# Reordering the prologue of a Fourier filter and mixer kernel: inputs first, tables and weights under the transposes, token sums among the roundings

## The chip, the cores and the metric

One core of one Trainium2 chip. The metric is the device time of one execution in microseconds (us); most kernels here ran five times beside runs of the kernel before on the same chip. All runs quoted are fast, with one core at a mean granted TensorE clock of 0.99. A ratio is the mean time of one kernel's fast runs over that of the other's of the same rounds, so it is not quite the ratio of the medians that are quoted. Times inside an execution ("the relu at 159.6") are from the profiled run, counted from the start of its span. In the profile's lines PE is TensorE, PEld its weight loads, DVE VectorE, ACT ScalarE, POOL GpSimd and SP SyncE; a q after the name means the engine's issuing side.

## The reference

```python
def _attn_ref(x, filt_r, filt_i):              # x: 8 x 3008 x 256, float32
    X = np.fft.rfft(x, axis=1)
    Y = X * (filt_r + 1j * filt_i)[None]       # filters: 1505 x 256
    return np.fft.irfft(Y, n=x.shape[1], axis=1).astype(np.float32)

def _moe_ref(x, w_tok1, w_tok2, w_ch1, w_ch2): # weights are float64
    h = np.maximum(x.transpose(0, 2, 1) @ w_tok1, 0.0) @ w_tok2
    u = x + h.transpose(0, 2, 1)
    return (u + np.maximum(u @ w_ch1, 0.0) @ w_ch2).astype(np.float32)
```

## The kernel before

The kernel does the first batch's Fourier filter in a prologue, and in the mixer it does the filters of later batches beside the matmuls. The weights arrive as float64, so each of 40 tiles is rounded to float32 in several steps: ScalarE makes the leading part, VectorE the rest, and the two parts are then added, either by VectorE or by two TensorE matmuls whose sum ScalarE copies out. One `convert()` ends one tile, copies for the next and starts a load for a later one.

```python
    early = [(up, "u")] * 2 + [(tp, "t")] * 2 + [(vp, "v")] * 2
    late = [(t2p, "t2"), (t3p, "t3")]
    stages = [(t4p, "t4")] * (A // 2) + early * 3 + late * 5   # staging buffer of each tile, in order
    ...
    def halves(st, n, pair):
        nc.scalar.activation(out=top, in_=hi_f, func=AF.Copy, scale=2.0 ** -112)
        yield
        ...                                     # four VectorE instructions -> top, rest
    def on_chip(stat, top, rest, n, parts):     # the sum by TensorE, put off by two roundings
        def f(tag=banks[0]):
            nc.tensor.matmul(ps[:, 0:n], stat, top, start=True, stop=False)
            nc.tensor.matmul(ps[:, 0:n], stat, rest, start=False, stop=True)
            for src, dst in parts:
                nc.scalar.copy(out=dst, in_=src(ps))
        behind.append((ended[0] - 1, f))
    def combine(w): ...                         # five GpSimd sums of channel weights
    def convert():
        ended[0] += 1
        while behind and behind[0][0] < ended[0] - 2:
            behind.pop(0)[1]()
        advance(end); advance(copy); advance(begin)
    ...
    # filter step k of the first batch; FB = 3 filter buffers, three parts of each filter by GpSimd's queue
            nc.tensor.matmul(ps, wbs[k // WC][...], t2, start=True, stop=True)
            nc.vector.tensor_tensor(out=p1, in0=ps, in1=fr, op=ALU.mult)
            ...                                 # two more products, then the inverse matmul of step k - 1
    ...
        for i in range(rounds, A // 2 + TC * N2 // NG):    # the last 14 roundings
            convert()
            ...
            if i == A // 2 + BY_PE - 1:
                sum_up()                        # flush the sums put off
                acc = token_sums(0)             # 96 matmuls in one block
        h1s[0] = token_relu(acc)
```

In all that follows each engine takes its instructions in the program's order, and the transfers of a queue stand in the order of the engine that issues them.

## Time and profile before

| | us |
|---|---|
| median of 3 runs | 2590.05 (2589.63 to 2591.91) |
| span of the profiled run | 2587.2 |
| TensorE busy from 222 us on | 2333.4 of 2365 |
| mixer's first matmul | 167.4 |

The mixer is at TensorE's limit from 222 us on, and the prologue ends at 167.4. The prediction below shows the stages and the chain of waits. Timeline columns: start, length, engine, source line, operation, output and input; in brackets how long the engine had been idle and what ended it.

### The profile page before, as it was taken

To read this page: it belongs to the slowest core of one execution; us is meant where nothing else is said; L and a number is where in the kernel's file an instruction comes from. 1 tells how busy PE (TensorE), PEld (TensorE's weight loads), DVE (VectorE), ACT (ScalarE), POOL (GpSimd) and SP (SyncE) were. 2 spreads that over 40 slices of the span, in tenths; PEclk is the share of its full clock that TensorE was granted. 3 is DMA by queue.
4 is the path that set the end of the run, shared out by engine and by line. 5 is a ranking of instruction groups with operands and counts; after the bars stand their busy time and mean duration, and the time that the engine had idled before them with its cause. 6 is when DMAs were issued, how large, how long until landed. Compare 5 with 4: busy or idle time off the path is not lost.

```text
span 2587.2 us, 31459 instructions
## 1 busy us (share of the span) xinstructions
PE 2505.6 (97%) x10952; PEld 2000.9 (77%) x10952; DVE 1816.0 (70%) x3458; ACT 691.2 (27%) x1347; POOL 526.9 (20%) x966
## 2 busy tenths in 40 slices
PE   5989999999999999999999999999999999999998
PEld 2556666788878777888787777788888888888887
DVE  6897888556675888746666788846678577647676
ACT  2433222123221222222321222212222122212222
POOL 3652211111211112112112111121121121211212
PEclk7999999999999999999999999999999999999999
DMA  6964333312232332202232233211232121100001
GB/s 167 232 195 155 109 106 103 106 48 90 90 90 64 88 88 71 80 17 89 90 96 77 75 84 87 80 31 57 90 85 75 50 64 53 25 9 8 17 12 21
DMA packets 151834, 205.20 MB, mean 79 GB/s; under 512 B 34216, under 2 KB 102034, under 8 KB 151676
## 3 DMA queue, kind: packets, MB, share of 16 engines
q1 hardware_dynamic: 81068, 115.65, 15.7%
q0 software_dynamic: 30656, 39.93, 6.4%
q10 hardware_dynamic: 39952, 47.61, 5.7%
q8 instruction: 87, 1.43, 0.2%
q14 instruction: 71, 0.58, 0.1%
HBM read 131.23 MB, written 71.83 MB: 78 GB/s over the span
## 4 chain that ended last, share of the span: by engine, by line
PE 78%; DVE 13%; issue 3%; DMA 3%; ACT 2%; SPq 0%; ACTq 0%; POOL 0%; DVEq 0%; POOLq 0%
PE ps_po L631 26%; PE ps_pg L597 15%; PE ps_pg L613 11%; PE ps_b L540 4%; PE ps_b L557 4%; DVE t L575 3%; DVE hh L575 3%; PE ps_acc L540 2%; PE ps_acc L557 2%; PE ps_acc L494 2%; PE ps_b L562 2%; PE ps_acc L417 2%; DVE u L575 2%; DVE s L575 1%; PE ps_b L470 1%
## 5 line engine op out<-in xcount | busy, mean ns | idle before, releaser
L575 DVE TENSOR_TENSOR hh<-ps_pg,s 128x512 f32<-128x512 f32 (+3 forms) x864 | 482.4, 586 | 624.4 <-ACT s L600 623.8
L676 POOL DMA_DIRECT2D out_dram<-r x757 | 409.8, 550 | 1949.1 <-ACT hh L618 929.0
L618 ACT ACTIVATE hh<-hh 128x512 f32<-128x512 f32 (+1 forms) x576 | 348.0, 621 | 1122.8 <-DVE hh L575 1122.8
L631 PE MATMUL ps_po<-t,wc 128*128 128x256 f32 (+1 forms) x2304 | 535.5, 375 | 5.4 <-DVE t L575 4.6
L631 PEld LDWEIGHTS ps_po<-t,wc 128*128 128x128 f32 x2304 | 434.5, 190 | 132.9 <-issue 53.3
L631 PE MATMUL ps_po<-hh,wc 128*128 128x256 f32 (+1 forms) x1728 | 413.2, 375 | 3.1 <-POOL wc L339 2.8
L597 PE MATMUL ps_pg<-v,wc 128*128 128x256 f32 (+1 forms) x1728 | 413.3, 375 | 0.2
L631 PEld LDWEIGHTS ps_po<-hh,wc 128*128 128x128 f32 x1728 | 327.5, 190 | 42.4 <-POOL wc L339 3.6
L597 PEld LDWEIGHTS ps_pg<-v,wc 128*128 128x128 f32 x1728 | 326.9, 190 | 40.5 <-DVE v L575 3.0
L613 PE MATMUL ps_pg<-u,wc 128*128 128x256 f32 (+1 forms) x1152 | 294.5, 378 | 7.0 <-DVE hh L575 6.5
L575 DVE TENSOR_TENSOR t<-t,hh 128x256 f32<-128x256 f32 (+1 forms) x576 | 242.0, 420 | 19.8
L613 PEld LDWEIGHTS ps_pg<-u,wc 128*128 128x128 f32 x1152 | 216.2, 190 | 43.5 <-DVE hh L575 17.4
L575 DVE TENSOR_TENSOR s<-ps_pg,hh 128x512 f32<-128x512 f32 (+1 forms) x288 | 196.0, 681 | 30.7 <-DVE hh L575 0.9
L575 DVE TENSOR_TENSOR t<-hh 128x512 f32<-128x512 f32 (+1 forms) x288 | 192.7, 669 | 0.6 <-ACT hh L618 0.6
L597 PE MATMUL ps_pg<-u,wc 128*128 128x256 f32 (+1 forms) x576 | 169.9, 377 | 1.6 <-DVE hh L575 1.6
L613 PE MATMUL ps_pg<-v,wc 128*128 128x256 f32 (+1 forms) x576 | 169.2, 375 | 0.0
L600 ACT COPY s<-ps_pg 128x256 f32<-128x256 f32 (+1 forms) x288 | 106.0, 368 | 154.7 <-PE ps_pg L597 151.5
L613 PEld LDWEIGHTS ps_pg<-v,wc 128*128 128x128 f32 x576 | 108.9, 190 | 13.3
L597 PEld LDWEIGHTS ps_pg<-u,wc 128*128 128x128 f32 x576 | 102.7, 191 | 20.3 <-issue 8.8
L540 PE MATMUL ps_b<-t,w 128*128 128x256 f32 x480 | 106.3, 384 | 4.3 <-DMA t<-g_tmp 4.3
L557 PE MATMUL ps_b<-w,h 128*128 128x512 f32 (+1 forms) x232 | 107.8, 587 | 0.0
L540 PEld LDWEIGHTS ps_b<-t,w 128*128 128x128 f32 x480 | 92.2, 192 | 17.9 <-issue 4.0
(102 smaller groups left out, 2251.4 us busy)
## 6 DMA issues: line engine op xcount, KB each, us to landing
g_tmp<-t ACTq DMA_DIRECT2D x128, 192.0 KB
x<-in_x_dram SPq DMA_DIRECT2D x184, 128.0 KB
out_dram<-r POOLq DMA_DIRECT2D x698, 32.0 KB, 1.8
z_tmp<-t ACTq DMA_DIRECT2D x84, 256.0 KB
t<-z_tmp SPq DMA_DIRECT2D x112, 192.0 KB
t<-g_tmp SPq DMA_DIRECT2D x42, 512.0 KB
wb<-wbi_t SPq DMA_DIRECT2D x80, 224.0 KB
filt<-in_filt_r_dram SPq DMA_DIRECT2D x128, 48.0 KB
```

Source lines behind the costliest of these rows:

```text
L417: nc.tensor.matmul(ps, wa0 if b == 0 else wa, xs.pop((b, c)).rearrange("p a d -> p (a d)"), start=True, stop=True)
L494: nc.tensor.matmul(ps[0:KR], wbs[k // WC][:, k % WC, P:], p, start=(i == 0), stop=(i == len(parts) - 1))
L540: nc.tensor.matmul(acc[:, t, :], w1[:, a, ts(t, P)], t4[b, a // TC4][:, a % TC4, :], start=(a == 0 and t == 0), stop=(a == A - 1 and t == ...
L557: nc.tensor.matmul(ps[:, 0:w], h1[:, t, ts(dh, P)], w2[:, t, ds(m * 512, w)], start=(t == 0), stop=False)
L562: nc.tensor.matmul(ps[:, ds(q * P, n)], t4[b, c][:, r, ts(dh, P)], wai[:, 0:n], start=False, stop=(q == 3))
L575: nc.vector.tensor_tensor(out=out, in0=in0, in1=in1, op=op)
L597: nc.tensor.matmul(ps[:, 0:hw], chan[0][:, jp, n, :], mov, start=True, stop=True)
L600: nc.scalar.copy(out=s[:, 0], in_=g[0][:, 0, 0:hw])
L613: nc.tensor.matmul(ps[:, 0:hw], chan[0][:, jp, n, :], mov, start=True, stop=True)
L618: nc.scalar.activation(out=hs, in_=hs, func=AF.Relu)
L631: nc.tensor.matmul(po[i][:, j, 0:hw], chan[1][:, jp, n, :], mov, start=(jp == 0 and first == 1), stop=(jp == JP - 1 and last == 1))
L676: q.dma_start(rows[g, e, :, ds(h * A + 4 * m, n)], blocks[ts(g, CW), h, e, 0:n])
```

## The change

Its intent: transfers idle under the transposes while the inputs ahead of them share the bandwidth with weights. So the inputs go first, in buffers of their own and over two queues; then seven tables; then weights, seven or more ahead. SyncE takes one part of each later filter load. The roundings that ran ahead of the transposes move beside the filter steps. The token sums are cut in eight parts among the last roundings, and TensorE adds twelve of the sixteen second token weight tiles, not six. The core of the diff:

```diff
-BY_PE = 6
-EARLY = 12
+BY_PE = 8
+BESIDE = 13
...
-                q.dma_start(t[lo + j0:lo + j0 + n, i, k - k0:KC, :],
+                (nc.sync if first and j0 and c >= FB else q).dma_start(t[lo + j0:lo + j0 + n, i, k - k0:KC, :],
...
+    round_ = [(p_, t_) for p_, t_ in ((up, "u"), (tp, "t"), (vp, "v"), (t2p, "t2")) for _ in range(2)]
+    stages = [(t4p, "t4")] * 7 + round_ * 3 + [(t2p, "t2"), (t3p, "t3")] * 5
...
-        q = nc.sync if i < EARLY else nc.gpsimd
+        q = nc.sync
...
-        if i < BY_PE:
+        if i < BY_PE or i % 2:
...
-        advance(begin)
+        while begun[0] < len(tiles) and begun[0] < ended[0] + (4 if begun[0] >= len(tiles) - len(LAST) else 7):
+            start()
...
-        where, tag = ((xp, "x"), (tp, "t"), (vp, "v"))[c % 3] if b == 0 else (xp, "x")
+        where, tag = ((xp, "x"), (t1p, "t1"), *round_[0::2])[c // 2] if b == 0 else (xp, "x")
+            q = nc.gpsimd if b == 0 and h else nc.sync
...
-        ahead = 3 * XB if first else XB
+        ahead = NXC if first else XB
+            if first and i < FB:
+                w_load(i)
+                if i == 0:
+                    for c in range(7):
+                        table_load(c)
...
+                if i >= FB:
+                    for _ in range(2 if i < 9 else 1):
+                        start()
...
-            if i == A // 2 + BY_PE - 1:
+            j = 3 * (i - A // 2 - TC * N2 // NG + 9)
+            if j == 0:
                 sum_up()
-                acc = token_sums(0)
+            if 0 <= j < A:
+                acc = token_sums(0, acc, range(j, j + 3))
+        sum_up()
```

More of the change, by code (lines that the diff above doesn't have):

```diff
@@ L34 @@
 KC = 2
-WC = 2
 DT = 256
@@ L225, in filt_double @@
         nc.scalar.copy(out=t[HALF:P, 0], in_=t[0:HALF, 0])
-    early = [(up, "u")] * 2 + [(tp, "t")] * 2 + [(vp, "v")] * 2
-    late = [(t2p, "t2"), (t3p, "t3")]
-    stages = [(t4p, "t4")] * (A // 2) + early * 3 + late * 5
+    round_ = [(p_, t_) for p_, t_ in ((up, "u"), (tp, "t"), (vp, "v"), (t2p, "t2")) for _ in range(2)]
+    stages = [(t4p, "t4")] * 7 + round_ * 3 + [(t2p, "t2"), (t3p, "t3")] * 5
     def stage(n):
@@ L378, in advance, with start @@
             next(s, None)
+    begun = [0]
+    def start():
+        advance(begin)
+        begun[0] += 1
     def sum_up():
@@ L405, in x_load @@
             lo = h * A + c * XC
-            nc.sync.dma_start(t[h * HALF:(h + 1) * HALF, 0:n, :], rows[:, lo:lo + n, :])
+            q = nc.gpsimd if b == 0 and h else nc.sync
+            q.dma_start(t[h * HALF:(h + 1) * HALF, 0:n, :], rows[:, lo:lo + n, :])
             if n < XC:
-                nc.sync.dma_start(t[h * HALF:(h + 1) * HALF, n:XC, :], rows[:, lo:lo + 1, :])
+                q.dma_start(t[h * HALF:(h + 1) * HALF, n:XC, :], rows[:, lo:lo + 1, :])
         xs[b, c] = t
@@ L429, in dft, with table_load @@
         wbs = {}
+        def table_load(c):
+            where, tag = ((xp, "x"), (t1p, "t1"))[(c - 3) // 2] if first and 3 <= c < 7 else (wbp, "wb")
+            wbs[c] = where.tile([P, KC, P + KR], FP32, tag=tag, name="wb")
+            nc.sync.dma_start(wbs[c], (wbi0_d if first else wbi_d)[:, ts(c, KC), :])
         def w_load(c):
-            if c * KC % WC == 0:
-                g = c * KC // WC
-                wbs[g] = wbp.tile([P, WC, P + KR], FP32, tag="wb", name="wb")
-                nc.sync.dma_start(wbs[g], (wbi0_d if first else wbi_d)[:, ts(g, WC), :])
+            if not first:
+                table_load(c)
             filt_load(c, first)
-        ahead = 3 * XB if first else XB
+        ahead = NXC if first else XB
         for u in todo[0:ahead]:
@@ L443, in dft @@
         for i, u in enumerate(todo):
-            if first and i in (5, 8):
-                w_load(i // 6)
+            if first and i < FB:
+                w_load(i)
+                if i == 0:
+                    for c in range(7):
+                        table_load(c)
             a_unit(*u)
@@ L469, in b_unit @@
             t2 = turned[:, k, :].unsqueeze(1) if first else t2s[k // KC][:, k % KC]
-            nc.tensor.matmul(ps, wbs[k // WC][0:P if first else KR, k % WC, 0:P], t2, start=True, stop=True)
+            nc.tensor.matmul(ps, wbs[k // KC][0:P if first else KR, k % KC, 0:P], t2, start=True, stop=True)
             re, im = slice(0, HALF), slice(HALF, P)
@@ L493, in bi_unit @@
             for i, p in enumerate(parts):
-                nc.tensor.matmul(ps[0:KR], wbs[k // WC][:, k % WC, P:], p, start=(i == 0), stop=(i == len(parts) - 1))
+                nc.tensor.matmul(ps[0:KR], wbs[k // KC][:, k % KC, P:], p, start=(i == 0), stop=(i == len(parts) - 1))
             c, r = divmod(k, KC)
@@ L517, in dft @@
                 b_unit(k)
-                if k % KC == 0 and k // KC + 2 < K2 // KC:
+                if k % KC == 0 and k // KC + 2 < K2 // KC and (k or not first):
                     t2_load(k // KC + 2)
                     w_load(k // KC + 2)
+                    for c in {2: (7,), 4: (8,), 6: (9,)}.get(k, (k // KC + 2,) if k >= 16 else ()):
+                        if first:
+                            table_load(c)
                 if first and k % KC == KC - 1 and k + 1 < K2:
@@ L534, in t4_load, with token_sums @@
         nc.sync.dma_start(t4[b, c][lo:hi], rows_of(g_d, b)[lo:hi, ts(c, TC4), :])
-    def token_sums(b):
-        acc = bank(free_bank()).rearrange("p (t d) -> p t d", t=TC)
-        for a in range(A):
+    def token_sums(b, acc=None, part=range(A)):
+        if acc is None:
+            acc = bank(free_bank()).rearrange("p (t d) -> p t d", t=TC)
+        for a in part:
             for t in range(TC):
@@ L771 @@
             nc.vector.memset(t, 0.0)
-        rounds = 0
         second = dft(GROUPS[1])
@@ L779 @@
             if i < NXC:
-                if i in (0, 2, 4, 6):
-                    advance(begin)
-                if i == 5:
+                if i >= FB:
+                    for _ in range(2 if i < 9 else 1):
+                        start()
+                if i == NXC - 1:
                     advance(copy)
-                if i in (7, 9, 11):
+            else:
+                k = i - NXC - 2
+                if k >= 0 and (k + 1) * BESIDE // (K2 + 1) > k * BESIDE // (K2 + 1):
                     convert()
-                    rounds += 1
-            else:
-                if (i - NXC) % 3 == 2:
-                    convert()
-                    rounds += 1
-                k = i - NXC - 2
                 if 19 <= k < 25:
                     t4_load(0, k - 19, 0, PARTS[1])
-                elif k == 25:
+                elif k == 28:
                     next(second)
@@ L805 @@
         chan.extend((both[:, 0], both[:, 1]))
-        for i in range(rounds, A // 2 + TC * N2 // NG):
+        acc = None
+        for i in range(BESIDE, A // 2 + TC * N2 // NG):
             convert()
-            if i - rounds < XB:
+            if i - BESIDE < XB:
                 next(second)
-            if i == A // 2 + BY_PE - 1:
+            j = 3 * (i - A // 2 - TC * N2 // NG + 9)
+            if j == 0:
                 sum_up()
-                acc = token_sums(0)
+            if 0 <= j < A:
+                acc = token_sums(0, acc, range(j, j + 3))
+        sum_up()
         h1s[0] = token_relu(acc)
```

## The prediction

> **What bounds the kernel now.** I read the page first, then a table of stretches cut at the program's stages, then the chain of waits and the timeline of the first 170 us. The page says TensorE is busy 97% of a 2587.2 us span. The table of stretches (one row each: stretch, length, busy time of each engine with instruction counts, granted TensorE clock, DMA share, GB/s) says where the other 3% is:
>
> ```profile
> 0.00:15.00 15.00, 7.52 (x12) 2.42 (x12) 4.50 (x4) 4.49 (x7) 10.51 (x24) 1.00 0.76 196
> 15.00:31.00 16.00, 10.37 (x13) 3.67 (x14) 6.72 (x12) 5.38 (x10) 0.55 (x1) 0.70 1.04 256
> 31.10:48.20 17.10, 1.80 (x4) 0.53 (x2) 17.00 (x16) 1.79 (x4) 0.00 (x0) 0.60 0.49 109
> 48.20:124.00 75.80, 69.44 (x239) 40.70 (x240) 65.29 (x144) 33.41 (x69) 48.14 (x87) 0.97 0.81 207
> 124.00:136.90 12.90, 9.45 (x26) 4.23 (x25) 9.47 (x22) 8.70 (x15) 2.76 (x5) 1.00 1.01 275
> 136.90:159.60 22.70, 22.64 (x96) 19.33 (x96) 21.53 (x46) 4.01 (x7) 10.55 (x20) 0.92 0.84 220
> 159.60:168.00 8.40, 7.72 (x30) 4.29 (x30) 6.34 (x12) 3.79 (x7) 2.59 (x5) 1.00 0.02 3
> 168.00:222.00 54.00, 43.09 (x157) 30.13 (x158) 49.38 (x86) 17.68 (x33) 39.65 (x64) 0.94 0.56 176
> 222.00:2587.00 2365.00, 2333.42 (x10379) 1895.65 (x10377) 1635.78 (x3121) 611.86 (x1198) 412.10 (x762) 1.00 0.24 69
> ```
>
> The stages: inputs and first Fourier step to 31; VectorE's sixteen transposes to 48; 32 filter steps with weight rounding beside them to 124; the rest of the rounding and the token sums to 160; then the mixer from about 167.4 on. From 222 on TensorE is busy 2333.4 of 2365 us, and the diff leaves that code as it is (the table tile is only renamed). So only the time until the mixer starts can move. All of it is 6.5% of the span, and 2% is 52 us, a third of it.
>
> The chain of waits of that prologue, in order of time (start, length, what):
>
> ```profile
> 8.20 5.17 DMA x<-in_x_dram
> 16.11 5.83 DMA st<-in_moe_w_tok_dram
> 23.15 5.15 DMA x<-in_x_dram
> 34.76 13.48 issue
> 128.96 3.34 DMA z_tmp<-t
> 132.29 4.50 DMA t<-g_tmp
> 136.93 22.66 PE ps_b L540 x96
> 159.61 0.61 ACT h L546
> ```
>
> The first stage is three transfers in a row: inputs share the 256 GB/s with weight tiles that nobody needs yet. The 13.48 us "issue" is the wait for the transposes, seen in the timeline:
>
> ```profile
> 31.14 17.00 DVE L455 STREAM_TRANSPOSE turned<-turned 128x512 f32<-128x512 f32 x16 [1.87 <-ACT turned L419]
> ```
>
> Transfers run at 109 GB/s under them, half of what they do before and after: the weight buffers are full. At the end the token sums wait for the last spectrum rows to go to memory and back, then 22.66 us of TensorE in one block, while VectorE rounds beside it (21.53 of 22.70). Both end together: VectorE's last token weight at 158.8, TensorE at 159.6.
>
> **What the Trainium skill says.** "DMA: Bandwidth & Descriptors", section "Issuing engines are not separate DMA queues": transfers from the scalar, sync and gpsimd queues run on the same 16 engines, and a second issuer saves only issue time. The trace agrees: both queues are busy at 15 to 31 us and the total is 256 GB/s. So splitting the input loads over two queues buys issue time (0.64 us from one SyncE load to the next), and the order of the bytes buys the rest. The same page, "Anatomy of one DMA — SWDGE (gpsimd) path": DMA engines do not wait on semaphores, the issuing sequencer does. So a load whose buffer isn't free blocks all behind it in its queue; SyncE issues nothing between 33.1 and 56.0 us here. "TensorE: Matmul & The Clock Gate", "Part 1: The HAM clock gate": the array clocks at half after idling and warms up after a few us of work. Here the granted clock is 0.60 in the transposes and 0.92 in the token sums that follow a 3.4 us wait.
>
> **The change part by part.**
>
> *Inputs first.* Before, the last of 12 input chunks lands at 28.4 us because 6 buffers are in flight and weights go between. After, all 12 have buffers and are issued first, lower halves by SyncE, upper halves by GpSimd. 12 SyncE issues at 0.64 us end at about 9 us; 13 GpSimd issues at about 0.55 us end at about 8. So bytes bind: 12 x 256 KB = 3.1 MB at the 256 GB/s of the second row is 12.1 us, from about 2.5 us (the first matmul ran at 4.59): 14.6, and about 1 us to land. One more chunk through TensorE (1.1 us) and ScalarE (0.59): transposes start at about 18 instead of 31.1. Saved: 13 us. They last 17.0 as before, to 35.
>
> *Tables and weights under the transposes.* Seven tables (7 x 224 KB = 1.6 MB), filters (0.6), 12 tiles of the first weight (6.2) and three of the second (1.2) follow: 9.6 MB or 37 us at 256 GB/s, to about 52 us. The hole under the transposes is filled. No filter step should then wait for a weight.
>
> *Filter steps.* VectorE's three products a step take 1.31 us apart (56.48 to 57.79), a rounding of a 512-wide tile 2.34 us (57.82 to 60.16). Before, three roundings ran ahead of the transposes, for free, and 11 beside the steps. Eight regular groups of three steps and a rounding (the spectrum matmul at 56.46 to the one at 107.95) take 6.44 us each; VectorE's own sum is 3 x 1.31 + 2.34 = 6.27. After, 13 roundings lie beside the steps and none before: 12 x 2.34 + 1.84 (a token weight of the second kind, 126.98 to 128.82) = 29.9, 32 x 1.31 = 41.9, and the same 0.17 us loss per rounding (2.2): 74.0. Before it was 74.4 from the first product at 49.5 to 123.9, where the eight groups' rate would give about 70: some 4 us went to late filters and tables at 108 to 117. I allow 1.5 us for that after, as transfers are saturated again in the last third: seven tiles ahead bring about 6.4 MB in the last 24 us. End at 35 + 1.3 + 74 + 1.5 = 112 instead of 124. Saved so far: 12 us.
>
> *The last roundings.* 15 instead of 14 remain. Rounded tiles added by TensorE cost VectorE 1.84 us, those added by VectorE 2.61 us (137.70 to 140.31). Before: 4 x 1.84 + 10 x 2.61 = 33.5. After, 11 and 4: 20.2 + 10.4 = 30.7. VectorE ends 14.8 us earlier than before. But TensorE takes 1.27 us for each tile that it adds (123.22 to 124.48).
>
> *Token sums in eight parts.* They start in the program after the seventh of these roundings and after the sums behind it are flushed: 112 + 7 x 1.84 + about 1.5 = 126.5. The spectrum rows come back 13.3 us after the last store was issued (123.65 to 136.93), so at about 125.5 if that latency stays. Either way 126 to 127 instead of 136.9. Then TensorE has 22.66 us of sums, a little less if the clock is full (the mixer's 256-column matmuls run at 1.73 us for 8 in the chain, 20.7 for 96), plus four additions of tiles among and after them, 5.1, plus ScalarE's last copy, about 0.8, before the relu. 126.5 + 21.5 + 5.9 = 154 instead of 159.6. VectorE is done with the token weights at 143 and with the first channel weights at 149, so TensorE sets the end here. Half of the gain goes back: the sums start 10 us earlier, but TensorE, no longer equal with VectorE, has the four additions in its way and the sums can't start before the flush.
>
> *Mixer.* From relu to start nothing changes (159.6 to 167.4). The first five items stay bound by VectorE with ten roundings (49.4 busy of 54). Perhaps 0.5 us as GpSimd's weight sums are ready at the start.
>
> Sum: 159.6 - 154 = 5.6, with 0.5 to 1: about 6.5 us. 2590 - 6.5 = 2583.5; I say 2583.
>
> **The rivals.**
> *The front's 13 us survive whole:* if TensorE is warm, the additions slip into gaps, and the reads come back sooner. For: TensorE is busy only 9.45 of 12.9 us in the stretch before the sums. Against: the table above adds up TensorE's work after the start of the sums, and none of it can move ahead of the spectrum. It would give 2577.
> *The return of the spectrum becomes the wait:* after, seven weight loads instead of four stand ahead in GpSimd's queue, and the stretch 124 to 137 is at 275 GB/s already. For: the last store and load took 13.3 us there. Against: no more bytes per us are asked for than before, one 377 KB load per rounding. If the sums start 4 us late: 2587.
> *Inputs aren't faster:* GpSimd's issue is slow, or tables and filters crowd in beside the inputs. Each queue then delays the transposes by 3 to 5 us: 2587 to 2589. Against: they stand behind the inputs in both queues.
> *VectorE stays the bound in the filter steps* through the roundings moved there: counted above; if each rounding costs the full sum of both engines' waits, 4 us more: 2587.
>
> **Range and chances.** Three of four rivals take 3 to 6 us away and one adds 6. Runs of before differ by 2.3 us. So 2583, and 2575 to 2589 eight times in ten. 2% is 52 us, more than all waiting in the prologue that the change can reach: faster by over 2% 0.01, within 2% 0.98, slower 0.01.
>
> **What would show it.** Transposes at 17 to 19 us (right if so; at 22 or later the inputs crowd); more than 200 GB/s under them; last filter step at 110 to 114; first token sum at 125 to 128, with its wait named (flush or returning rows); eight blocks of 12 matmuls with additions between; relu at 152 to 156; the mixer from 222 on equal within 1 us when shifted. The prediction is wrong if the relu is before 148 or after 160, or if the mixer's rows change in length.

## More of the kernel before

```profile
155.60 1.45 POOL L345 DMA_DIRECT2D st<-in_moe_w_ch_dram  x3 [2.38 <-issue]
165.17 0.53 POOL L335 TENSOR_SCALAR wc<-wc 128x128 f32<-128x128 f32 x1 [8.11 <-DVE wc L273]
...
167.71 0.52 POOL L339 TENSOR_TENSOR wc<-wc 128x128 f32<-128x128 f32 x1
```

The channel loads that the mixer starts with are issued by 157.1; then GpSimd waits for VectorE's rounded weights and sums them at once, and the mixer's second group of matmuls starts at 168.06.

## The result, and the profile after

The changed kernel took 2600.81 us in the median of 4 runs (2600.29 to 2601.95), the kernel before 2589.84 in the same rounds: ratio 1.0044, 95% interval 1.0027 to 1.0062. It is 11 us slower. The forecast had been 7 us faster, and its range ended at 2589.

The table of stretches of the changed kernel, cut at its own milestones (columns as in the prediction; the engines are PE, PEld, DVE, ACT, POOL):

```profile
0.00:19.70 19.70, 13.38 (x24) 4.61 (x24) 4.50 (x4) 8.20 (x13) 14.97 (x32) 1.00 0.92 245
19.70:36.80 17.10, 0.00 (x0) 0.00 (x0) 17.00 (x16) 1.83 (x4) 5.03 (x10) 0.58 1.05 265
36.80:122.90 86.10, 68.83 (x236) 40.62 (x237) 68.27 (x148) 33.16 (x68) 30.64 (x57) 0.92 0.73 184
122.90:139.50 16.60, 16.34 (x43) 6.88 (x41) 13.07 (x31) 10.86 (x19) 4.00 (x8) 1.00 0.97 259
139.50:166.10 26.60, 25.95 (x113) 21.09 (x111) 16.82 (x37) 7.23 (x16) 5.04 (x10) 1.00 0.32 98
166.10:178.40 12.30, 7.72 (x30) 4.28 (x30) 10.19 (x18) 4.77 (x9) 6.70 (x12) 1.00 0.46 129
178.40:222.00 43.60, 36.15 (x124) 25.03 (x125) 39.37 (x67) 14.96 (x27) 35.93 (x59) 0.91 0.58 180
222.00:2599.00 2377.00, 2343.30 (x10411) 1901.87 (x10409) 1641.96 (x3132) 613.38 (x1202) 414.38 (x767) 1.00 0.24 69
```

The hole under the transposes is full (265 GB/s against 109), and they start at 19.7 in place of 31.1. But the filter stage, 36.8 to 122.9, is 86 us long with VectorE busy 68 of it. Its loss is in one place, as finer cuts of the same table show:

```profile
38.20:48.00 9.80, 8.38 (x31) 4.77 (x30) 9.27 (x22) 2.77 (x6) 4.26 (x8) 0.93 0.85 207
48.00:60.20 12.20, 0.44 (x3) 0.04 (x1) 2.65 (x5) 0.59 (x1) 2.27 (x4) 0.72 0.94 215
60.20:75.00 14.80, 13.72 (x45) 8.43 (x46) 12.10 (x27) 7.35 (x16) 4.88 (x10) 0.89 0.32 85
```

From 48 to 60.2 the engines stand almost still (VectorE from 50.8 on) while transfers run at 215 GB/s. The changed kernel's view of who waited for whom in 38 to 62 us (total, times, longest; L224 is the doubling of a filter, L497 VectorE's first product), and below it SyncE's timeline of issues, name the cause:

```profile
ACT filt L224 <- DMA filt<-in_filt_r_dram: 12.8, 1, 12.8
...
DVE p L497 <- ACT filt L224: 9.5, 1, 9.5
```
```profile
17.79 33.66 SPq L300 DMA_DIRECT2D st<-in_moe_w_tok_dram  x24
51.63 0.40 SPq L219 DMA_DIRECT2D filt<-in_filt_r_dram  x1
```

ScalarE needs the fourth filter to double it, and one part of that filter is issued by SyncE behind 24 weight loads. Those take 33.66 us to issue, 1.40 us each on average, although their buffers were free when the last input matmul ended at 19.1. What SyncE waited for in 17 to 52 us (same columns; L300 is a weight load, `g_tmp<-t` ScalarE's store of spectrum rows):

```profile
SPq L300 <- DMA st<-in_moe_w_tok_dram: 12.6, 9, 4.0
SPq L300 <- DMA g_tmp<-t: 6.5, 1, 6.5
```

In this program the transfers of SyncE and ScalarE take turns at eight completion semaphores, and each waits until the one eight places before it has landed. So a line of loads moves at the pace of earlier transfers, and not of weights alone: the eighteenth load stood from 40.3 to 46.87 for a store that the first filter steps produce. Six more loads followed, then the filter part at 51.63; it landed at 59.5, behind their bytes.

At the handover GpSimd's timeline has changed too:

```profile
171.39 4.05 POOL L344 DMA_DIRECT2D st<-in_moe_w_ch_dram  x8 [23.97 <-ACT top L244]
175.59 0.72 POOL L334 TENSOR_SCALAR wc<-wc 128x128 f32<-128x128 f32 x1
```

GpSimd stood 24 us on a load whose staging buffer wasn't free, then issued eight loads in 4 us, and only then summed the weights that the mixer begins with. The mixer's second group starts at 178.44, where it was 168.06.

At the very end GpSimd's five last stores are interrupted in the changed kernel's timeline (the kernel before issues its five in one piece of 2.71 us):

```profile
2591.55 0.55 POOL L695 DMA_DIRECT2D out_dram<-r  x1 [13.50 <-issue]
2594.63 2.17 POOL L695 DMA_DIRECT2D out_dram<-r  x4 [2.54 <-issue]
```

So there are three candidates for lost time, and beside them the price of the additions that TensorE took over. The theories to test were: the two queues' order (filter part on SyncE, channel loads on GpSimd); rivals, the bandwidth itself, and ScalarE's late roundings; and for the token sums, the splitting against the additions.

### The profile page after: what moved, and what is told of

Read it like the earlier page. It is cut to its first block, busy times and chain, and to the rows that moved or that the text cites. A ratio compares the mean times of both kernels' runs of the same rounds, so it can differ in the third digit from the quotient of the medians.

```text
span 2599.4 us, 31530 instructions
## 1 busy us (share of the span) xinstructions
PE 2511.7 (97%) x10976; PEld 2004.4 (77%) x10976; DVE 1811.2 (70%) x3450; ACT 694.4 (27%) x1355; POOL 516.7 (20%) x953
## 3 DMA queue, kind: packets, MB, share of 16 engines
q0 software_dynamic: 30416, 41.13, 6.5%
## 4 chain that ended last, share of the span: by engine, by line
PE 77%; DVE 13%; issue 2%; ACT 2%; DMA 1%; ACTq 1%; POOL 0%; DVEq 0%; SPq 0%; POOLq 0%
PE ps_po L650 26%; PE ps_pg L616 15%; PE ps_pg L632 11%; PE ps_b L559 4%; PE ps_b L576 4%; DVE t L594 3%; DVE hh L594 3%; PE ps_acc L559 2%; PE ps_acc L576 2%; PE ps_b L581 2%; PE ps_acc L509 2%; DVE u L594 2%; PE ps_acc L425 2%; DVE s L594 1%; PE ps_b L509 1%
## 5 line engine op out<-in xcount | busy, mean ns | idle before, releaser
L594 DVE TENSOR_TENSOR t<-t,hh 128x256 f32<-128x256 f32 (+1 forms) x576 | 242.1, 420 | 19.8
L619 ACT COPY s<-ps_pg 128x256 f32<-128x256 f32 (+1 forms) x288 | 105.8, 367 | 159.2 <-PE ps_pg L616 155.3
L509 PE MATMUL ps_acc<-p,wb 128*96 128x256 f32 (+1 forms) x256 | 95.9, 474 | 20.6 <-ACT t L515 13.8
```

Of the source, the lines that this page charges most:

```text
L509: nc.tensor.matmul(ps[0:KR], wbs[k // KC][:, k % KC, P:], p, start=(i == 0), stop=(i == len(parts) - 1))
L594: nc.vector.tensor_tensor(out=out, in0=in0, in1=in1, op=op)
L619: nc.scalar.copy(out=s[:, 0], in_=g[0][:, 0, 0:hw])
```

## The experiments

There were seventeen runs, with the one of the prediction; all results were correct. Unless said otherwise each is an edit of the changed kernel. Rounds were shared in four groups; medians of before in them were 2587.74, 2588.89, 2589.54 and 2588.94, so a difference between runs of two groups is good to some 2 us only.

**First group: the two queues.**

Filter part back on GpSimd's queue:

```diff
-                (nc.sync if first and j0 and c >= FB else q).dma_start(t[lo + j0:...
+                q.dma_start(t[lo + j0:...
```

> The third part of each filter load goes back from SyncE's queue to GpSimd's, all else as in the changed kernel. Queue theory (the part stood behind 24 weight loads in SyncE's queue, so VectorE idled 50.8 to 60.3 us): the idle stretch goes, first token sum some 8 to 9 us earlier than the changed kernel's 139.5, time about 2592. Bandwidth rival (the weight tiles fill the transfer engines until 51 us, whoever issues the filter part): the stall stays within 2 us of its 9.5 and the time at 2599 to 2601.

Measured: 2588.59, ratio 1.0005 (0.9992 to 1.0018). First sum at 130.8, relu at 157.4. The wait is gone (1.0 us is left) although the same bytes move; so the order in the queue caused it, not the bandwidth. The gain was 3 us larger than expected; the fourth group says why.

Staging order of the last tiles, so that the next loads don't need a buffer still in use:

```diff
-    stages = ... + [(t2p, "t2"), (t3p, "t3")] * 5
+    stages = ... + ([(t3p, "t3")] * 2 + [(t2p, "t2")] * 2) * 3
```

> Only the staging buffers of the last ten weight tiles are taken in another order (two of the one pool, two of the other, in place of turn by turn), so that the loads of tiles 31 and 32 need not wait for the rounding of tile 29 in GpSimd's queue. Queue theory for the mixer's start (GpSimd issued eight loads for 4 us ahead of the sums of the first channel weights, 171.4 to 175.4): those sums start near 171.7, TensorE's wait of 3.95 us for them falls under 1 us, the time falls by about 4 to 2597. Rival (ScalarE's late rounding of the channel weights at 164.8 and 166.6 sets the start by itself): the wait stays near 4 us, the time within 1 us of 2601.

Measured: 2599.06 (2596.77 to 2600.16), ratio 1.0042. In the trace the weight sums start at 171.3 and the mixer's second group at 174.2, as the queue theory has it; the medians gave under 2 us from other rounds than the changed kernel's. It was run again below.

Both edits:

> Both edits at once. If the two delays lie one after the other on the path they add: about 2588, equal to the kernel before within 3 us. If one hides the other: no better than the better of the two single edits.

Measured: 2586.61, ratio 0.9995 (0.9983 to 1.0008). They add, and the time is inside the prediction's range (up to 2589). But it equals the kernel before within noise (1.1 us less), where 6.5 us had been forecast.

Token sums in one block, twelve additions kept:

```diff
-            if 0 <= j < A:
-                acc = token_sums(0, acc, range(j, j + 3))
+                acc = token_sums(0)          # under `if j == 0`, after the flush
```

> Token sums in one block again, at the place where the first of the eight parts stood; TensorE's tile additions stay at twelve. Theory that the interleaving costs (ScalarE's copies of added tiles wait behind parts of the sums and hold up the roundings behind them in its queue, VectorE idles 4.9 us at 147.6 to 152.5): the roundings of the channel weights come late all the same, since all additions now wait for the whole block; time 2600 to 2605. Rival (splitting itself costs, in switching between sums and additions): 2596 or less.

Measured: 2609.67, 9 us slower than the changed kernel and 4.7 beyond the upper end of what was expected; relu at 175.4. VectorE's waits in 140 to 176 us:

```profile
DVE both L246 <- ACT both L244: 15.2, 1, 15.2
```

Additions, ScalarE's copies of them, ScalarE's next rounding step and VectorE stand in a ring, and one block of 20.7 us in TensorE's order holds the whole ring. So with twelve additions the eight parts are needed.

**Second group: the token sums, on top of both queue edits**, and one from the changed kernel.

TensorE adds the first eight tiles only:

```diff
-        if i < BY_PE or i % 2:
+        if i < BY_PE:
```

> On top of both queue edits, TensorE adds only the first eight token weight tiles; the odd ones after them go back to VectorE. Theory (TensorE sets the end of the token sums, and each addition costs it 1.27 us): the relu comes 4 to 5 us earlier than the 155.4 with both edits alone, at about 151, VectorE ending its token weights at about 149; time about 2582. Rival (VectorE takes over as the bound: 4 x 0.77 us more for it and nothing gained): relu at 154 or later, time within 1 us of 2586.6.

Measured: 2580.78, ratio 0.9969 (0.9956 to 0.9981); relu at 149.5, VectorE without one wait from 128 to 150. The four late additions cost 6 us, a little more than expected.

The same with the sums in one block:

> As the last, and the sums in one block in place of eight parts. If one block was bad only because additions, ScalarE's copies and the roundings behind them stood in a ring, it costs nothing here, where no addition comes after the block: relu and time within 1 us of the last run. If splitting is worth something by itself (the 9 us of the one-block run with twelve additions), it is 3 us or more slower.

Measured: 2579.94, ratio 0.9967 (0.9955 to 0.9980). Splitting is worth nothing where no addition follows.

Sums begun two roundings earlier, no flush, twelve additions:

```diff
-            j = 3 * (i - A // 2 - TC * N2 // NG + 9)
-            if j == 0:
-                sum_up()
+            j = 3 * (i - A // 2 - TC * N2 // NG + 11)
```

> On top of both queue edits (twelve additions kept), the eight parts begin two roundings earlier and the flush of waiting additions ahead of them is left out. If the flush holds the sums up (rows back at about 125, first sum at 128.8): sums start at 125 to 126 and the relu comes 1 to 3 us earlier, time 2584 to 2586. Rival (TensorE is full from the last filter step on, so order doesn't matter): relu within 0.7 us of 155.4.

Measured: 2591.19, slower by 4.6 than with both edits (of other rounds). Both expectations missed: the sums began at 122.3, 6.5 us earlier and earlier than I had thought the rows to be back, but the relu came at 158.2. The ring again, now six times over (VectorE's waits in 122 to 158 us):

```profile
DVE both L246 <- ACT both L244: 9.5, 6, 1.9
```

The changed kernel with nine tiles ahead under the transposes, filter part still on SyncE:

```diff
-                    for _ in range(2 if i < 9 else 1):
-                        start()
+                    start()
```

> The changed kernel with the filter parts still on SyncE's queue, but nine weight tiles issued under the transposes in place of fifteen, so 18 loads stand ahead of the first filter part and not 24. Queue theory: at 1.4 us a load the first part is issued some 8 us earlier (51.6 to about 43), VectorE's 9.5 us wait for it falls under 3, time 2590 to 2594. Rival (the wait is due to something else in the filter loads' move, as the short rows read by SyncE): the wait stays at 8 us or more, time 2599 to 2601.

Measured: 2592.34, ratio 1.0016. The first filter part was issued at 46.45 and not 43: the last of the 18 loads stood 9.0 us for the same store of ScalarE. Yet no wait of VectorE over 1 us is left between 43 and 60. So a shorter line ahead of the filter part cures the same wait from the other side.

**Third group: the changed kernel beside single edits, and a best version.**

> The changed kernel once more, unedited, so that it and the next two share their rounds. Expected 2600 to 2602, first token sum at 139 to 140, relu at 166, the mixer's second group of matmuls at 178.

Measured: 2602.11, ratio 1.0050; first sum at 140.4, relu at 166.95, second group at 179.3.

> The staging order edit alone again, beside the changed kernel in the same rounds. In the trace it brought the mixer's second group of matmuls from 178.4 to 174.2; the medians, from different rounds, gave 2 us. If the 4 us last to the end: 4 us (3 to 5) under the changed kernel. If the mixer's first items take half of it back: 1.5 to 2.5 us.

Measured: 2599.55, ratio 1.0038: 2.6 us less than its neighbour. The mixer's second group came 3.5 us earlier (175.8), the relu of the mixer's second batch 2.7 us. The first items of the mixer took back about a quarter, which lies between the two theories.

Eight additions, both queue faults left in:

> The changed kernel with both queue faults left in, and TensorE adding eight tiles, not twelve. If the four additions cost the end of the sums as much here as with the queue edits (155.4 to 149.5 for the relu): relu at about 160.3, time about 2595. Rival (hidden behind the two queue faults): within 1.5 us of 2601.

Measured: 2595.00, ratio 1.0019, 7.1 us less than its neighbour; relu at 162.2, two later than expected. The additions cost as much here, so they aren't hidden behind the faults.

Both queue edits, six additions, one block two roundings earlier:

```diff
-BY_PE = 8
+BY_PE = 6
-            j = 3 * (i - A // 2 - TC * N2 // NG + 9)
+            j = 3 * (i - A // 2 - TC * N2 // NG + 11)
```

> A candidate for the best: both queue edits, six tiles added by TensorE as before the change, sums in one block two roundings earlier (the rows were back by 122.3 in the early-sums run). Sums start at 123 to 126 in place of 130, VectorE becomes the last with its token weights at about 148, relu at 146 to 148; time 2576 to 2579, against 2580 for eight tiles. If VectorE gives it all back: 2580 to 2582.

Measured: 2581.17. Sums at 125.1 and relu at 146.0 as expected, but the mixer's second group at 159.2, against 157.8 with eight: VectorE, last with its tiles, gives it all back. Eight is about the balance.

**Fourth group: the pause at the end.** In each of the seven traces until then whose filter part is on SyncE (30416 packets on GpSimd's queue) the last five stores have it, always 2.54 us and after the first of them, and in none of the other seven (30656 or 31248 packets).

> The changed kernel unedited, as the measure for the next three: 2600 to 2603, with the pause of 2.5 us in GpSimd's last stores.

Measured: 2602.05, pause as before.

> The filter part back on GpSimd, in the same rounds as the changed kernel. From the traces: the relu 8.7 us earlier (166.1 to 157.4) plus the 2.5 us pause that this kernel doesn't have, so 10 to 12 us under the changed kernel. If the pause costs nothing: 8 to 9.

Measured: 2589.31, 12.7 us less, a little more than expected. At the mixer's last relu the two traces differ by 9.7 us, and by 12.4 at the end.

Last stores on two queues, without GpSimd:

```diff
-   q = (nc.sync, nc.scalar, nc.gpsimd)[(h * 8 + e * 4 + g) % 3] if last else nc.gpsimd
+   q = (nc.sync, nc.scalar)[(h * 8 + e * 4 + g) % 2] if last else nc.gpsimd
```

> The changed kernel with its last sixteen stores on SyncE and ScalarE alone, eight each. If GpSimd's pause sets the end: stores issued within 3.7 us of each other and the end 1 to 2.5 us earlier, time 2599 to 2601. If the end was set by SyncE's stores anyway: within 0.5 us, or 1 us later.

Measured: 2598.70, 3.3 us less. From the first of the last stores to the end it is 6.1 us (2590.81 to 2596.9) against 8.4 in its neighbour (2589.82 to 2598.2). So the pause is worth about 2.3 us of the 3.3 (the edit also moves five stores to other queues); the rest is within the spread of runs.

Forty small GpSimd instructions added in the mixer:

```diff
+            if (b, i, place) == (3, 2, 0):
+                for _ in range(40):
+                    nc.gpsimd.memset(idle, 0.0)
```

> The changed kernel with 40 small memsets added on GpSimd in the mixer's fourth batch, where it is mostly idle; no transfer is added. If the pause comes at fixed places of GpSimd's instruction stream, it moves off the last five stores: no pause there, end 2 to 3 us earlier, 2598 to 2600. If it goes with the number of transfers on its queue: the pause of 2.54 us stays where it is and the time within 1 us of the changed kernel.

Measured: 2600.82; the pause stays, 2.54 us after the first store. So it isn't bound to a place in GpSimd's instruction count. The rest of the traces tells what it is bound to. Such pauses stand all along GpSimd's stores, in the kernel before too (the first line is from it, the second from the changed kernel):

```profile
2567.02 2.71 POOL L676 DMA_DIRECT2D out_dram<-r  x5 [1.73 <-issue]
1321.10 2.17 POOL L695 DMA_DIRECT2D out_dram<-r  x4 [2.54 <-issue]
```

Counted along the queue, they come every 108 transfers once only stores are left on it: after transfer 236, 344, 452, 560, 668, 776 and 884 of the changed kernel's 888, after 459, 567, 675 and 891 of 901 in the kernel before, and after 463, 571, 679, 787 and 895 of 914 with the filter part back on GpSimd. They take 1.5 to 2.6 us. With loads moved between queues the pauses fall elsewhere, in the changed kernel one among the last stores, where nothing hides it; the run with the last stores on two queues ends at transfer 883 and escapes it. What the queue does in a pause stays open.

## Why the prediction was wrong

Milestones in us, from the traces. "Roundings beside" is the end of the last rounding placed beside the filter steps.

| | before | predicted | changed | both queue edits | and eight additions |
|---|---|---|---|---|---|
| transposes start | 31.1 | 18 | 19.7 | 19.8 | 20.4 |
| roundings beside end | 124.1 | 112 | 122.9 | 112.2 | 112.0 |
| first token sum | 136.9 | 126.5 | 139.5 | 128.8 | 128.6 |
| relu | 159.6 | 154 | 166.1 | 155.4 | 149.5 |
| mixer's second group | 168.1 | 162 | 178.4 | 163.8 | 157.8 |
| span | 2587.2 | | 2599.4 | 2583.6 | 2577.9 |

The prediction's entry for the mixer is its relu plus the 8.5 us of before, less its 0.5.

*Inputs first.* Mechanism right, size off by 1.7 us. Transfers ran at 245 GB/s in that stretch, not 256, and shared it with filters and tables. SyncE's twelve input loads were issued by 14.3 and not 9, since they too waited for earlier landings (2.2 us for a table that ScalarE loads). The rival of slow inputs (3 to 5 us) did not happen.

*"No filter step should then wait for a weight."* This is the step that failed. It counted the bytes (to end at about 52 us; the last of these weights landed at 59.3) and said that buffers ahead make waits vanish. No step waited for a weight; one waited for a filter that stood behind weights. The diff line that moves a third of each filter load to SyncE was given no place in the sum, although the prediction itself cited that a load blocks all behind it in its queue. Where 94 us were worked out from the transposes' start to the end of these roundings, it took 103.2, with VectorE's 9.5 us wait in it; with the line undone and the staging order mended, 92.4. Two readings of the old trace were off as well. For the slow transfers under the transposes it named full weight buffers; what SyncE stood for there, 22.2 us (33.8 to 56.0), was the buffer of a table, with weight loads behind it. And "both queues are busy at 15 to 31 us" isn't so: GpSimd's queue had 3.9% of the transfer engines' time there. That two queues share the rate is shown by the changed kernel, where they moved 2.7 and 1.8 MB in the first 19.7 us at 245 GB/s in all.

*The last roundings.* 16.6 us from there to the first sum, in the versions with the flush at that place (16.9 with nine tiles ahead), where 14.5 was worked out: VectorE waits 1.6 and 1.2 us for ScalarE in the first two tiles, which also copies two input units there. A mis-sized term. The second rival (rows coming back late) is refuted: with the sums begun earlier they started at 122.3 without waiting for rows.

*Token sums.* 26.6 us from first sum to relu, 27.5 predicted. That TensorE sets this end and that four additions cost it some 5 us was right: undoing them gave 6 to 7 us. The chain of waits of the changed kernel shows the additions between the sums:

```profile
139.66 10.36 PE ps_b L559 x48
150.02 0.63 PE ps_po L283 x2
150.66 0.63 PE ps_po L284 x2
151.29 5.18 PE ps_b L559 x24
```

*Mixer: "From relu to start nothing changes", perhaps 0.5 us gained.* Wrong: 12.4 us to the second group and not 8.5. Loads were now ahead of GpSimd's sums in its queue. With the staging order mended it is 8.5 (155.37 to 163.84). The mixer's first items gave part of the loss back: 10.4 us late at their start, the changed kernel was 8.4 us late at the next batch's relu.

*The end.* The pause, some 2.3 us, was in no step. The profile of before has one 14 us ahead of its last stores; it was not asked where the next kernel's would fall.

Sum of the misses, changed against predicted: 1.7 inputs, 9.2 filter stage, 2.1 flush, -0.9 sums, 4.4 handover (12.4 against 8.0), -2.0 given back in the first items, 1.1 drift up to the last relu, 2.7 at the end: 18.3 us. The medians are 17.8 apart (2600.8 against 2583). Some two thirds of it (9.5 and 4.4, less the 2.0) stand in two queues where a load was put ahead of something more urgent.

The rival "the front's 13 us survive whole" was wrong too: 11.4 us at the transposes were 11.9 at the end of the roundings with both edits, 8.1 at the first sum, 4.2 at the relu. The loss between the last two is the additions. Without them the version with both queue edits and eight tiles is the best measured: 2580.8, or 2579.9 with one block of sums, 8 to 9 us faster than before (0.3%).

## What to carry to other kernels

When a change moves a load to another queue or issues more loads ahead, write down for each queue the order of everything in it and when the loads ahead can be issued. A load waits not only for its buffer but for earlier transfers to land, in this program even for a store of another engine; free buffers don't help what stands behind it. Look at GpSimd the same way where it both loads and computes: a load that waits for its buffer delays the sums behind it. Give an engine more additions only after asking which of the engines ends that stage last, and whether its results stand in a ring with the copies and roundings that feed it.

## What the Trainium skill lacked or had wrong

- "DMA: Bandwidth & Descriptors", "Issuing engines are not separate DMA queues": it says that a second issuer only saves issue time, usually small. Which queue carried one part of a filter load decided a wait of 9.5 us and, with the pause, 12.7 us of the time, because of what stood ahead in that queue.
- The same page, "Anatomy of one DMA — SWDGE (gpsimd) path": that waits happen at the issuing sequencer is right and explains both queue faults. It doesn't say how far a queue issues ahead: with eight completion semaphores for SyncE and ScalarE together, SyncE needed 33.66 us for 24 weight loads, 6.5 of them for one store of ScalarE's, where the kernel before issued two such loads in 1.10 us (at 56.47).
- No page has the pauses of 1.5 to 2.6 us in GpSimd's queue, which in these traces come every 108 stores.
